# An mLSTM layer and its feed-forward block on one core: two groups' down projections change from float32 to divided float32r words, and the written order is new

## The chip, the cores and the metric

The kernel runs on one core of one Trainium2 chip. The metric is the device time of one execution in microseconds (us), the median of several runs. TensorE is called PE in the profile, its weight loads PEld, VectorE DVE, ScalarE ACT, GpSimd POOL, SyncE SP. All DMAs of the kernel are issued from SP's queue, in the order in which they are written.

## What is computed

Inputs are q, k, v and o_gate of shape (4, 8, 768, 40) and i_gate, f_gate of shape (4, 8, 768). For every batch and head, over the 768 time steps:

```
m_new = max(f + m, i);  f_stab = exp(f + m - m_new);  i_stab = exp(i - m_new)
C = f_stab * C + i_stab * outer(v, k);   n = f_stab * n + i_stab * k
y = sigmoid(o) * (C q) / max(|n q|, 1)
```

The result, as 3072 tokens of 320 values, goes through a feed-forward block with w_in (320 x 2048) and w_out (2048 x 320):

```
h = x @ w_in;   g = h * erf(softplus(h));   out = g @ w_out
```

The weights arrive as 64-bit words and are decoded on the chip.

## The kernel before

The sequence is cut into 12 chunks of 64 steps. For a chunk c, `attention` (line 414) works on two sides r of two batches each. For each side a scores step on PE (function `scores`, line 498), a heads step (`heads`, line 522) with the carried state (`before`, line 507), and short DVE steps give the chunk's y. The decay matrix `dm` is made for chunks 0 and 1 from a matmul `pb` (line 442) and an exponential on ACT (line 447); its operands are `lt` (line 338) and `xd` (lines 346 and 348), built once from the gates. Later chunks read the gates back from DRAM. `turned` (line 384) transposes y, `divided` (line 393) splits it into two float32r words, xh and xl, so that xh + xl is y.

The feed-forward block of a chunk's 256 tokens is done in four groups of 512 hidden columns, 48 groups in all, by `mlp(g)` (line 714). Groups 0 to 7 are those of chunks 0 and 1, alternating: groups 0, 2, 4, 6 are chunk 0's, 1, 3, 5, 7 chunk 1's. A group has two up steps of 16 matmuls (four of 5 from group 16 on), line 746, whose results ACT copies to `hb` (line 757); softplus and erf on ACT (lines 766, 770) and a product on DVE (line 774) give `n0`. Its down projection adds to two PSUM tiles, one for each half b of the tokens. It has two forms:

- undivided, for groups under PLAIN: for each half four float32 matmuls of n0 with the decoded w_out block `wo` (line 810). Each such matmul is recorded as two instructions.
- divided, for the other groups: `gh` is n0 in float32r (on ACT, line 784, for groups under 32), `gl` what is left of n0 (on DVE, line 790); w_out is divided into `woh` and `wol` by `split_out` (lines 707 and 711). For each half there are four matmuls gh x woh, four gh x wol (lines 814 and 815) and four gl x woh (line 812), in two steps of their own.

Nothing of this is ordered where it stands in the code: `Plan.add` records every step with its engine and what it reads and writes, and `Plan.run` issues the steps in a written list, `ORDER`, of the steps' numbers. Each engine executes its own steps in that order. A negative number -n in `ORDER` is a stay round: `stay(n)` issues n matmuls whose result is not used. `run` also puts in a load of an ACT function table (recorded at line 873) wherever a step on ACT needs a table that isn't loaded.

PSUM tiles of tag `pa` have two slots that are taken in turn by the steps of attention, the transposes and the down projections of chunk 1; `h` has two slots for up projections.

Of the kernel before, what the change touches and what calls it, by code (L numbers as in the profile page):

```python
# [33 lines left out]
class Plan:  # L34
# [131 lines left out]
PLAIN, JOIN, GH_ACT = 6, 3, 32  # L166
# [3 lines left out]
def tile_mlstm_moe(  # L170
# [43 lines left out]
    wl = cp.tile([128, 2, DFF], F32R, name="wl")  # L214
    woh = cp.tile([128, NFF, DM], F32R, name="woh")

    accs = []
    pob = [ps.tile([128, 512], F32, name=f"pob{b}") for b in range(2)]

    @dma(6, w=[('cst', 0)])  # L220
# [714 lines left out]
```

## Time and profile before

| | us |
|---|---|
| median of 3 runs | 464.68 (464.56 to 464.76) |
| the profiled execution | 462.74 |
| its span in the trace | 461.0 |
| PE busy | 450.4 |
| PE's weight loads busy | 402.8 |
| DVE busy | 330.7 |
| ACT busy | 336.9 |

The span is the time from the first to the last recorded event of the profiled execution. An engine's busy time is the time in which at least one of its instructions ran; ends of matmuls are modelled. The granted clock of PE is its mean over the span, 0.987 of full speed.

### The profile page before, as it was taken

What the parts mean: (1) busy time and instruction counts of PE and PEld (TensorE: products, weight loads), DVE (VectorE), ACT (ScalarE), POOL (GpSimd) and SP (SyncE); (2) the same over time, 40 slices, a digit from 0 to 9 for tenths busy, and PEclk for the clock granted to TensorE, in tenths of its full rate; (3) what the DMA queues carried; (4) which work ended last, traced back from release to release, by engine and by line L of the source; (5) the groups of instructions that cost most, each with busy time, mean ns of one, the idle gap of its engine ahead of it and who ended that gap; (6) DMA issues with size and microseconds to landing.
All of it is one profiled execution on the core that took longest, in us unless ns stands there. A gap on an engine that the chain in (4) does not pass through costs nothing.

```text
span 461.0 us, 14089 instructions
## 1 busy us (share of the span) xinstructions
PE 450.4 (98%) x6102; PEld 402.8 (87%) x6102; DVE 330.7 (72%) x655; ACT 336.9 (73%) x529; POOL 37.2 (8%) x62
## 2 busy tenths in 40 slices
PE   6989999999999999999999999999999999999996
PEld 4568998798889998999999899898899899999996
DVE  5879787857769477686868768858759876666491
ACT  4737999988878975786876895698596573575570
POOL 2000121020500200031000200102002000000000
PEclk9969999999999999999999999999999999999999
DMA  7999898923442141525317211672122300001011
GB/s 270 319 290 271 224 261 234 249 99 92 96 125 66 42 108 24 164 68 169 84 37 229 63 26 43 176 208 68 45 77 70 77 1 14 16 1 30 2 28 30
DMA packets 46831, 51.82 MB, mean 112 GB/s; under 512 B 27056, under 2 KB 31664, under 8 KB 46768
## 3 DMA queue, kind: packets, MB, share of 16 engines
q1 hardware_dynamic: 46768, 50.91, 39.8%
q8 instruction: 48, 0.79, 0.7%
q14 instruction: 15, 0.12, 0.1%
HBM read 46.77 MB, written 4.13 MB: 110 GB/s over the span
## 4 chain that ended last, share of the span: by engine, by line
PE 93%; DVE 3%; ACT 1%; issue 1%; DMA 0%; DVEq 0%
PE h L746 39%; PE pob L812 11%; PE pob L814 11%; PE pob L815 10%; PE pa L528 4%; PE pob L810 3%; PE pa L810 3%; PE pa L514 3%; PE pa L505 3%; PE pa L519 2%; PE pa L387 2%; PE pob L281 1%; PE pob L870 1%; PE pa L391 1%; DVE raw L633 1%
## 5 line engine op out<-in xcount | busy, mean ns | idle before, releaser
L746 PE MATMUL h<-xh,wh 128*128 128x256 f32 (+1 forms) x768 | 201.8, 345 | 0.2 <-ACT hb L757 0.2
L746 PEld LDWEIGHTS h<-xh,wh 128*128 128x128 f32 x768 | 126.5, 190 | 14.2 <-ACT hb L757 0.4
L757 ACT ACTIVATE hb<-h 128x256 f32<-128x256 f32 (+1 forms) x160 | 66.5, 423 | 66.0 <-PE h L746 65.2
L746 PE MATMUL h<-xh,wl 128*128 128x256 f32 x384 | 108.3, 282 | 0.0
L814 PE MATMUL pob<-woh,gh 128*128 128x320 f32 x328 | 98.3, 311 | 0.0
L815 PE MATMUL pob<-wo,gh 128*128 128x320 f32 x328 | 97.5, 309 | 0.0
L762 DVE TENSOR_TENSOR hb<-h,hb 128x256 f32<-128x256 f32 x128 | 52.6, 421 | 53.0 <-ACT hb L757 52.2
L873 ACT ACT_TABLE_LOAD x61 | 78.3, 1283 | 1.9 <-PEq L923 0.8
L746 PEld LDWEIGHTS h<-xh,wl 128*128 128x128 f32 x384 | 72.9, 190 | 2.2
L774 DVE TENSOR_TENSOR n<-n,hb 128x1024 f32<-128x1024 f32 x48 | 58.8, 1226 | 9.5 <-ACT n L770 9.5
L815 PEld LDWEIGHTS pob<-wo,gh 128*128 128x128 f32 x328 | 61.6, 188 | 1.5
L814 PEld LDWEIGHTS pob<-woh,gh 128*128 128x128 f32 x328 | 61.7, 188 | 0.4
L812 PE MATMUL pob<-woh,gl 128*128 128x320 f32 x328 | 61.7, 312 | 0.0
L483 POOL TENSOR_SCALAR_AFFINE_SELECT dm<-dm 128x512 f32<-128x512 f32 (+1 forms) x40 | 33.8, 851 | 310.9 <-ACT dm L463 229.4
L766 ACT ACTIVATE n<-hb 128x1024 f32<-128x1024 f32 x48 | 50.0, 1056 | 5.5 <-DVE hb L762 4.7
L812 PEld LDWEIGHTS pob<-woh,gl 128*128 128x128 f32 x328 | 52.3, 188 | 1.9
L790 DVE TENSOR_TENSOR gl<-n,gh 128x1024 fp32r<-128x1024 f32 x42 | 51.0, 1219 | 1.2 <-PE pob L815 0.4
L770 ACT ACTIVATE n<-n 128x1024 f32<-128x1024 f32 x48 | 49.9, 1055 | 0.3
L404 DVE TENSOR_TENSOR xh<-pa,xh 128x384 fp32r<-128x384 f32 x24 | 13.2, 551 | 23.1 <-ACT xh L400 23.0
L784 ACT ACTIVATE gh<-n 128x1024 fp32r<-128x1024 f32 x26 | 27.2, 1053 | 0.0
L560 DVE TENSOR_TENSOR dm<-pa,dm 128x512 f32<-128x512 f32 x24 | 16.4, 685 | 10.7 <-PE pa L505 7.6
L820 ACT ACTIVATE o<-pob 128x320 f32<-128x320 f32 x22 | 9.5, 437 | 17.4 <-PE pob L812 17.4
(97 smaller groups left out, 484.6 us busy)
## 6 DMA issues: line engine op xcount, KB each, us to landing
qk<-in_qk_dram SPq DMA_DIRECT2D x24, 512.0 KB
kvo<-in_kvo_dram SPq DMA_DIRECT2D x24, 484.0 KB
eT<-gd SPq DMA_DIRECT2D x44, 128.0 KB
raw<-in_w_out_dram SPq DMA_DIRECT2D x16, 320.0 KB
dm<-gd SPq DMA_DIRECT2D x40, 128.0 KB
raw<-in_w_in_dram SPq DMA_DIRECT2D x8, 512.0 KB
out_dram<-o SPq DMA_DIRECT2D x48, 80.0 KB
raw<-in_w_in_dram SPq DMA_DIRECT2D x4, 256.0 KB
```

Of the source, the lines that this page charges most:

```text
L483: nc.gpsimd.affine_select(out=x, in_=x, pattern=[[0, H], [1, L]], compare_op=ALU.is_ge, fill=0.0, base=base, channel_multiplier=-1)
L746: nc.tensor.matmul(h[:, n * T:n * T + n_], w, m, start=(s == 0), stop=(s == len(ops) - 1))
L757: nc.scalar.activation(part(), G(f'h{i}')[:, T:2 * T] if wide else G(f'h{i}'), AF.Copy)
L762: nc.vector.tensor_tensor(part(), G(f'h{i}')[:, 0:T], part(), op=ALU.add)
L766: nc.scalar.activation(new('n0', [128, 1024], ('n0', g)), G('hb'), AF.Softplus)
L770: nc.scalar.activation(G('n0'), G('n0'), AF.Erf)
L774: nc.vector.tensor_tensor(G('n0'), G('n0'), G('hb'), op=ALU.mult)
L790: nc.vector.tensor_tensor(new('gl', [128, 1024], ('gl', g), F32R), G('n0'), G('gh').bitcast(F32), op=ALU.subtract)
L812: nc.tensor.matmul(acc(b), G('gl')[:, ts], woh[:, j], start=False, stop=(j == NFF - 1))
L814: nc.tensor.matmul(acc(b), G('gh')[:, ts], woh[:, j], start=(j == 0), stop=False)
L815: nc.tensor.matmul(acc(b), G('gh')[:, ts], t['wol', j], start=False, stop=False)
L873: plan.run(ORDER, lambda k: nc.scalar.preload_act_table_set(KIND[k]), stay)
```

## The change

PLAIN goes from 6 to 4, so that the down projections of groups 4 and 5 take the divided form, and the division of w_out's blocks 8 to 11 is needed by them. ORDER is replaced as a whole; it has 1595 steps in place of 1587, numbered anew, and stay rounds that add up to six, as before. A stay round that comes before any down projection now multiplies the identity if that has been made, and the zeroed state otherwise, so that it can stand ahead of the step that makes the identity.

```diff
 ORDER = [
-    1, 2, 0, 5, 9, 4, 6, 12, 13, 14, 3, 10, 7, 15, 16, 99, 101, 20, 31, 8, 17, 11, 33, 100, 102, 32, 34, 36, 35, 27, 28, 93,
-    95, 19, 38, -1, 40, 42, -2, 47, 341, 342, 18, 26, 30, 48, 343, 49, 50, 94, 96, 103, 67, -1, 68, 25, 37, 24, 39, 105, 23,
...
+    1, 4, 0, 3, 5, 7, 9, 11, 12, 6, 13, 2, 14, 15, 16, 8, 17, 33, 27, 32, 34, 36, 35, 20, 19, 31, 38, -1, 40, 28, 26, 29, 93,
+    95, 349, 350, 351, 42, -2, 47, 94, 48, 49, 18, 67, 68, 99, 96, 10, 50, 59, 60, 25, 37, 30, 39, 52, 65, 23, 100, 101, 102,
...
 ]
-PLAIN, JOIN, GH_ACT = 6, 3, 32
+PLAIN, JOIN, GH_ACT = 4, 3, 32
...
-    accs = []
+    accs, made = [], []
...
         make_identity(nc, ident)
+        made.append(ident)
...
-                nc.tensor.matmul(pob[1], ident, ident.unsqueeze(1).to_broadcast([128, 4, 128]), start=True, stop=True)
+                x = made[0] if made else state[0].rearrange("p j n d -> p (j n d)")[:, 0:128]
+                nc.tensor.matmul(pob[1], x, x.unsqueeze(1).to_broadcast([128, 4, 128]), start=True, stop=True)
```

Read through the step numbers, the first PE steps are, with pb, S, H for the decay matmul, scores and heads, the chunk and the side behind them, T for transposes, A for the transposition of the gates (line 358) and up for an up step:

```
old: warm pb01 pb00 S01 stay1 H01 stay2 pb11 stay1 S00 pb10 T01 H00 stay1 S11 S10 stay1 T00 A  H11 up0 up2 up2
new: warm pb01 pb00 S01 stay1 H01 stay2 pb11 pb10 S00 T01 H00 stay2 S11 S10 stay1 A T00 H11 up0 up2 up2
```

The first ACT steps around the exponentials of line 447 are:

```
old: ... exp01 tanh01 exp00 decode(i00) xd state01 lt decode ...
new: ... exp01 tanh01 exp(gates) xd exp00 tanh00 decode(i00) state01 lt ...
```

The down projections of groups 0 to 7 stand further apart in the new list: groups 0 and 2 first, then up steps of groups 8 to 11, then groups 1, 3, 5 and 7 close together, then 4 and 6.

## Rows read from the trace of the kernel before

**Rows 1.** The page's first part: busy us, share of the span, instructions.

```profile
PE 450.4 (98%) x6102; PEld 402.8 (87%) x6102; DVE 330.7 (72%) x655; ACT 336.9 (73%) x529; POOL 37.2 (8%) x62
```

**Rows 2.** Windows: stretch, length, busy us by engine, PE clock, DMA share, GB/s.

```profile
0.00:44.00 44.00, 37.46 (x674) 26.50 (x674) 32.72 (x79) 24.81 (x56) 3.37 (x22) 0.88 0.97 288
44.00:457.00 413.00, 412.96 (x5430) 376.32 (x5429) 297.96 (x578) 311.62 (x472) 33.78 (x40) 1.00 0.35 94
...
0.00:126.00 126.00, 119.42 (x1873) 98.69 (x1874) 95.35 (x217) 100.43 (x172) 18.11 (x38) 0.96 0.78 218
...
455.00:461.00 6.00, 2.00 (x14) 1.73 (x12) 0.00 (x0) 0.57 (x2) 0.00 (x0) 0.89 0.25 55
```

**Rows 3.** Waits of PE over the whole span: total us, times, longest.

```profile
PE pob L281 <- DVE sel L258: 3.6, 1, 3.6
PE pa L505 <- issue: 1.9, 1, 1.9
```

**Rows 4.** Windows of 1 us around 25 to 38 us.

```profile
24.00:25.00 1.00, 0.00 (x0) 0.00 (x0) 0.94 (x2) 0.00 (x0) 0.00 (x0) 1.00 1.01 397
...
26.00:27.00 1.00, 1.00 (x2) 0.30 (x2) 1.00 (x2) 0.00 (x0) 0.00 (x0) 0.62 1.07 427
...
37.00:38.00 1.00, 1.00 (x11) 1.00 (x10) 0.91 (x5) 0.85 (x3) 0.00 (x0) 1.00 1.01 308
```

**Rows 5.** PE's timeline, undivided down projections and what follows: start, us.

```profile
67.21 2.32 PE L810 MATMUL pob<-wo,n 128*128 128x320 f32 x8
69.46 0.69 PE L505 MATMUL pa<-qk 40*64 40x64 f32 x32
...
90.08 4.57 PE L810 MATMUL pa<-wo,n 128*128 128x320 f32 x16
94.50 0.53 PE L358 MATMUL pa<-ident,x 128*128 128x32 f32 x4
```

**Rows 6.** PE's timeline, first of 12 divided matmuls and what follows them.

```profile
98.61 0.31 PE L814 MATMUL pa<-woh,gh 128*128 128x320 f32 x1
...
100.38 0.40 PE L746 MATMUL h<-xh,wh 128*128 128x256 f32 x2
```

**Rows 7.** Groups by line: busy us, mean ns, idle before.

```profile
L873 ACT ACT_TABLE_LOAD x61 | 78.3, 1283 | 1.9 <-PEq L923 0.8
...
L790 DVE TENSOR_TENSOR gl<-n,gh 128x1024 fp32r<-128x1024 f32 x42 | 51.0, 1219 | 1.2 <-PE pob L815 0.4 <-PE pob L812 0.4 <-ACT gh L784 0.3
...
L784 ACT ACTIVATE gh<-n 128x1024 fp32r<-128x1024 f32 x26 | 27.2, 1053 | 0.0
```

**Rows 8.** ACT's timeline from 9.6 us.

```profile
9.69 0.60 ACT L447 ACTIVATE dm<-pa 128x512 f32<-128x512 f32 x1 [1.21 <-PE pa L442]
10.18 0.46 ACT L488 ACTIVATE kvo<-kvo 128x320 f32<-128x320 f32 x1
10.54 0.60 ACT L447 ACTIVATE dm<-pa 128x512 f32<-128x512 f32 x1
...
11.59 2.01 ACT L346 ACTIVATE xd<-x,heads_of 128x64 f32<-128x64 f32 x8
```

**Rows 9.** PE's timeline: heads steps, a decay matmul, a scores step's last part.

```profile
12.12 0.66 PE L519 MATMUL pa<-vg,kvo 64*64 64x41 f32 x32
...
17.71 1.13 PE L442 MATMUL pa<-xd,lt 128*128 128x512 f32 x2
...
19.88 0.66 PE L519 MATMUL pa<-vg,kvo 64*64 64x41 f32 x32
...
25.50 0.34 PE L505 MATMUL pa<-qk 40*64 40x64 f32 x6 [1.92 <-issue]
```

**Rows 10.** PE's timeline in the first up step, 12 matmuls between the two.

```profile
33.54 0.41 PE L746 MATMUL h<-xh,wl 128*128 128x256 f32 x1
...
36.10 0.41 PE L746 MATMUL h<-xh,wh 128*128 128x256 f32 x1
```

**Rows 11.** The chain that ended last, in order of time: one later up step.

```profile
74.15 1.91 PE h L746 x16
```

137 rows, old and new, of the table ORDER are left out of this document.

## The prediction

> **What bounds the kernel now.** I read the shares of the engines first. TensorE (PE) is busy for 98% of the span, VectorE (DVE) and ScalarE (ACT) for some 72% [rows 1]. An average can hide a stage with another limit, so next come the windows [rows 2]: from 44 to 457 us PE is busy for 412.96 of 413 us at full granted clock. Before 44 it is busy 37.46 of 44 us at a mean clock of 0.88, with the DMA engines 97% busy. After 457 comes only the last eviction and its store: PE is busy 2.00 of the last 6 us. "Busy" is a modelled duration for pipelined matmuls, so the windows alone don't show that PE works at its peak; the distances between the starts of matmuls do, in the part below. The waits of PE [rows 3] add up to 6.4 us, all before 44 us; the two largest are shown, and one is the wait for the first data. The other, 1.9 us, waits for nothing that the profile shows. So two things set the time: how long PE's own list of work takes from 44 us on, and how soon, and at which clock, PE gets going before that.
>
> The 1 us windows show the opening's weak place [rows 4]. PE does nothing from 24 to 25 us, the granted clock is 0.62 in 26 to 27, stays at its lower level (0.50, 1.2 GHz), and is back at 1.00 in 37 to 38.
>
> **The change, part by part.**
>
> *Removed and added on PE.* Groups 4 and 5 lose their undivided down projections. The undivided form is 8 float32 matmuls of 320 columns a group, each recorded as two instructions. Group 5 ran as one block of 16 instructions from 90.08 to 94.50, 4.42 us. Group 4 ran in halves; a half of 8 instructions takes 2.25 us (67.21 to 69.46, that of group 0), so 4.50 us [rows 5]. Together 8.92 us. In their place come 12 float32r matmuls for each half of the tokens: 8 with gh (lines 814, 815) and 4 with gl (line 812). Group 7 did such a half from 98.61 to 100.38, 1.77 us [rows 6]; four halves are 7.08 us. The difference is 8.92 - 7.08 = 1.84 us less on PE, 0.92 a group. PE has no idle time there, so I count all of it. Its bounds: 1.76 if both groups had cost 4.42, 1.92 if both had cost 4.50.
>
> The Trainium skill (FP8 and Floating Point Precision, TensorE Precision Notes) says that true float32 takes four passes through the array. By that rule alone three single passes in place of four would save a quarter of 8.92, 2.2 us, and the time would be 462.4; the rows say 1.84, since a float32r matmul takes somewhat more than a quarter of a float32 one.
>
> *Added on ACT and DVE.* Two more gh copies on ACT at 1.053 us, two more gl subtractions on DVE at 1.219 us [rows 7]. Following both written orders through the planner's rule for activation tables gives 61 loads for the old order, as many as the trace has, and 54 for the new one: seven fewer, at 1.283 us 9.0 us less on ACT [rows 7]. ACT thus loses 9.0 - 2.1 = 6.9 us net, DVE gains 2.4. Neither engine is the bound after 44 us, so I cost both at nothing. What hides them is PE's full list; what it costs when that cover is gone is a rival below. The steps that divide w_out are the same 16; those of blocks 8 to 11 only move ahead of group 4's and 5's projections.
>
> *The order of the opening.* Up to the first up projection both orders give PE the same steps, five stay rounds included, and ask for the same qk, kvo and w_in loads, within some 16 KB. Two things differ. First, the exponential of the second side's decay (line 447) ran on ACT at 10.54, before the 2.01 us that build the second half of xd; the new order puts it behind them and behind another tanh [rows 8]. Counted from the first exponential's end: 10.29 + 0.46 + 2.01 + 0.60 = 13.36. The first heads step needs the PSUM slot that this exponential frees, and started at 12.12 [rows 9]. It will start about 1.2 us later. Second, the new order puts pb of the fourth side directly behind that of the third, ahead of the scores, and drops one stay round between them, so a step that PE did late before (17.71) now fills what was a wait. I reckon that the lag has shrunk by the heads step at 19.88, but can't price it exactly: its bounds are 0 and 1.2 us. Then comes PE's gap, whose end (25.50, the last 6 matmuls of a scores step of 32 pairs) no data releases [rows 9]: it falls inside one step whose first 26 pairs had run, and the new order reaches it after the same PE steps. I expect it again, at nearly the same time, and hiding what is left of the lag. So I take 0.
>
> *pA2 ahead of the transposes.* In the new order the small transposition of the gates (line 358) precedes the transposes of chunk 0's second side. The next step then takes its PSUM slot after a short ACT copy instead of after the division by ACT and DVE. PE waited only 0.2 us there, so this gives at most 0.2; I take 0.
>
> *The first groups.* For its second pair of up projections the new order wants w_in's second tail as well, because DVE decodes it earlier: about 0.5 MB more than before. At the 288 GB/s of the first 44 us [rows 2] that is 1.8 us of transfer, but later steps want about 1 MB less than before at the same place. PE is doing the first up projection meanwhile. Bounds: 1.8 lost, nothing lost; I take nothing.
>
> *The end.* After group 47's last up projection the new order leaves PE twelve pieces of down projection (groups 44 to 46, 3 x 3.54 = 10.6 us) before it needs group 47's. The old order leaves as much. No change.
>
> Sum: 464.68 - 1.84 = 462.84, say 462.8. The profiled execution took 462.74 (span 461.0, with 1.7 around it), 1.94 below the median of the runs; I add the difference to the median, and for a profiled run of the new kernel would expect 460.9.
>
> **The rivals.**
>
> *The opening becomes shorter.* At the lower clock the up projection's matmuls started every 0.213 us (12 of them from 33.54 to 36.10 [rows 10]); at the higher one a step of 16 takes 1.91 us, 0.119 each [rows 11]. So an up step costs 1.5 us more at the lower clock. If the activity before 26 us changes so that the clock falls later or returns one step earlier, 462.84 - 1.5 = 461.3; with one and a half steps 460.6. For it: the new order closes gaps between 15 and 19 us. Against: the gap at 24 us has the same PE steps before it.
>
> *The lag of 1.2 us is carried through.* Then 464.0, and with a further wait for the second tail up to 465.6: no measurable change. For it: ACT's list really has the 2.01 us in front. Against: PE's later gap is longer than the lag.
>
> *DVE falls behind between 90 and 130 us; slower.* The new order packs DVE's work tighter there: eight divisions of w_out and the gl of groups 5 and 7 come close together. Adding the mean durations of all DVE instructions that stand in the new order ahead of what the scores of chunk 4's first side need, scaled by 0.92 so that a whole kernel's sum equals DVE's busy time, gives 100.1 us. PE's list puts those scores at 127.5, so DVE may have idled 27.4 us by then. The old kernel's DVE had idled 126 - 95.35 = 30.65 us by 126 [rows 2], its order allowing 33.7. If DVE idles as it did, PE waits 3.3 to 3.5 us: 462.84 + 3.5 = 466.3. It decides from 2.8 us of waiting on. Against: DVE idled mostly waiting for ACT, and ACT has fewer table loads now; the same count for ACT leaves 27.6 us or more where the old kernel idled about 25.6 [rows 2].
>
> *The lower clock lasts two up steps longer; slower, barely.* Two steps at 1.5 are 3.0 us: 465.8. This happens if PE idles again between 33 and 40 us, waiting for w_in. The windows show what precedes a fall: a microsecond without matmuls, then 0.62 [rows 4]. The Trainium skill (TensorE: Matmul & The Clock Gate, Part 1) says that the clock is released by PE's activity and taken back when it idles; the trace agrees, with 0.00 us of PE work in 24 to 25 and 0.50 soon after.
>
> **How the numbers follow.** Forecast (1.84 less, the opening even to within 0.9): 0.46, 461.9 to 463.7. Shorter opening: 0.17. Lag carried: 0.20. DVE late: 0.11. Lower clock longer: 0.06. This kernel's runs lie within 0.05% of each other; 0.2%, 0.93 us, is about what can be told from no change. Faster by more than that, below 463.75: 0.46 + 0.17 = 0.63. Within it: 0.20. Slower, above 465.61: 0.17. The range runs from 460.6 (a shorter opening by one and a half steps) to 466.3 (DVE late by 3.5); some 0.15 lies outside.
>
> **What would show it.** Right: 32 fewer float32 down instructions (line 810), 64 in all; 54 table loads; PE busy in practically every window after 46 us; the last matmul some 1.8 us earlier; a gap without a releaser in the second scores step of chunk 1 near 25 us, with the clock falling after it. Wrong: PE waits named DVE or ACT between 60 and 140 us, or a first dense stretch that starts more than 1 us before or after 44.

## The result, and the profile after

The changed kernel takes 459.06 us (median of 4 runs, 458.40 to 460.07), against 464.62 before: ratio 0.9882, 95% interval 0.9863 to 0.9901. It is 5.6 us faster; 1.84 was forecast, and 459.06 lies below the range. The profiled execution took 458.40 with a span of 456.7, 4.3 less than before. The rest up to 5.6 is the old kernel's profiled execution lying 1.9 below its median, the new one's 0.7. All lines of the code stand two or three further down now (746 is 748, 810 is 812, 505 is 507, 528 is 530, 873 is 876).

The page's first part, and from its third part PE's instruction queue (packets, MB, share):

```profile
PE 445.6 (98%) x6118; PEld 401.6 (88%) x6118; DVE 336.5 (74%) x657; ACT 328.5 (72%) x524; POOL 37.3 (8%) x62
...
q8 instruction: 48, 0.79, 0.7%
```

Windows of the changed kernel, with columns as in [rows 2]:

```profile
0.00:44.00 44.00, 37.13 (x702) 27.36 (x703) 35.12 (x86) 28.36 (x63) 3.34 (x22) 0.96 0.88 281
...
40.50:456.70 416.20, 411.96 (x5457) 377.71 (x5445) 304.62 (x580) 303.64 (x469) 33.96 (x40) 1.00 0.34 97
...
29.00:30.00 1.00, 0.05 (x5) 0.04 (x7) 0.97 (x3) 0.84 (x2) 0.00 (x0) 1.00 0.63 156
31.00:32.00 1.00, 1.00 (x9) 1.00 (x8) 0.97 (x2) 0.86 (x2) 0.00 (x0) 0.65 0.75 251
37.00:38.00 1.00, 1.00 (x11) 1.00 (x10) 0.94 (x3) 0.92 (x2) 0.00 (x0) 1.00 0.99 399
```

PE was as busy in the first 44 us as before, but at a mean clock of 0.96 in place of 0.88 [rows 2]. The dense stretch begins near 40.5, not at 43.9. Waits of PE over the whole span (total, times, longest):

```profile
PE pob L283 <- DVE state L272: 3.6, 1, 3.6
PE pa L530 <- issue: 1.8, 1, 1.8
PE pa L507 <- issue: 0.9, 2, 0.7
PE h L748 <- DVE wl L649: 0.2, 1, 0.2
```

The one wait of 1.9 us without a releaser [rows 3] has become several, of which PE's timeline shows the two largest; it answers to [rows 9]:

```profile
11.59 0.66 PE L521 MATMUL pa<-vg,kvo 64*64 64x41 f32 x32
...
18.48 0.66 PE L521 MATMUL pa<-vg,kvo 64*64 64x41 f32 x32
19.07 0.81 PE L530 MATMUL pa<-kvo,dm 64*32 64x41 f32 x64
...
22.03 1.11 PE L507 MATMUL pa<-qk 40*64 40x64 f32 x58 [0.23 <-issue]
23.84 0.34 PE L507 MATMUL pa<-qk 40*64 40x64 f32 x6 [0.70 <-issue]
...
27.47 0.65 PE L530 MATMUL pa<-kvo,dm 64*32 64x41 f32 x46
29.95 0.38 PE L530 MATMUL pa<-kvo,dm 64*32 64x41 f32 x18 [1.83 <-issue]
30.26 0.51 PE L748 MATMUL h<-xh,wh 128*128 128x256 f32 x2
```

I cut both traces at the same work: the start of the first up matmul, the start of the fourth up step (the same steps lie before it in both), and the start of the last block of gl matmuls.

| us | before | after | difference |
|---|---|---|---|
| gap inside the two scores steps ends | 25.50 | 23.84 | -1.66 |
| first up matmul | 32.95 | 30.26 | -2.69 |
| fourth up step | 43.94 | 40.53 | -3.41 |
| last gl block | 456.25 | 451.91 | -4.34 |
| from the fourth up step to the last gl block | 412.31 | 411.38 | -0.93 |

Each trace is one execution. So 3.41 of 4.3 us came ahead of the stretch for which the prediction counted a gain, from a part it costed at nothing. After that it is 0.93, not 1.84. These are the two things to explain.

### The profile page after: what moved, and what is told of

Its sections match the earlier page's. It is cut to its first block, busy times and chain, and to the rows that moved or that the text cites. A ratio compares the mean times of both kernels' runs of the same rounds, so it can differ in the third digit from the quotient of the medians.

```text
span 456.7 us, 14133 instructions
## 1 busy us (share of the span) xinstructions
PE 445.6 (98%) x6118; PEld 401.6 (88%) x6118; DVE 336.5 (74%) x657; ACT 328.5 (72%) x524; POOL 37.3 (8%) x62
## 4 chain that ended last, share of the span: by engine, by line
PE 92%; DVE 3%; ACT 2%; DMA 1%; issue 1%; SPq 0%; DVEq 0%
PE h L748 40%; PE pob L816 11%; PE pob L814 11%; PE pob L817 11%; PE pa L530 3%; PE pa L507 3%; PE pa L516 3%; PE pa L812 2%; PE pob L812 2%; PE pa L521 2%; PE pa L389 2%; PE pa L444 1%; PE pob L873 1%; DMA eT<-gd 1%; DMA gt<-in_gates_dram 1%
## 5 line engine op out<-in xcount | busy, mean ns | idle before, releaser
L816 PE MATMUL pob<-woh,gh 128*128 128x320 f32 x336 | 101.1, 313 | 0.0
L817 PE MATMUL pob<-wo,gh 128*128 128x320 f32 x336 | 100.1, 310 | 0.0
L817 PEld LDWEIGHTS pob<-wo,gh 128*128 128x128 f32 x336 | 63.2, 188 | 1.4
L816 PEld LDWEIGHTS pob<-woh,gh 128*128 128x128 f32 x336 | 63.2, 188 | 0.5
L814 PE MATMUL pob<-woh,gl 128*128 128x320 f32 x336 | 62.7, 312 | 0.0
L792 DVE TENSOR_TENSOR gl<-n,gh 128x1024 fp32r<-128x1024 f32 x44 | 53.9, 1228 | 2.2 <-ACT gh L786 1.9
L814 PEld LDWEIGHTS pob<-woh,gl 128*128 128x128 f32 x336 | 53.5, 188 | 2.0
L786 ACT ACTIVATE gh<-n 128x1024 fp32r<-128x1024 f32 x28 | 29.5, 1052 | 0.0
L530 PEld LDWEIGHTS pa<-kvo,dm 64*32 64x32 f32 x1536 | 16.7, 106 | 5.9 <-issue 5.0
```

The lines of the kernel that those rows point to most:

```text
L792: nc.vector.tensor_tensor(new('gl', [128, 1024], ('gl', g), F32R), G('n0'), G('gh').bitcast(F32), op=ALU.subtract)
L814: nc.tensor.matmul(acc(b), G('gl')[:, ts], woh[:, j], start=False, stop=(j == NFF - 1))
L816: nc.tensor.matmul(acc(b), G('gh')[:, ts], woh[:, j], start=(j == 0), stop=False)
L817: nc.tensor.matmul(acc(b), G('gh')[:, ts], t['wol', j], start=False, stop=False)
```

## The experiments

All kernels compute the whole reference. The old kernel ran beside them on other chips: 464.3 to 464.6 us in the median, single runs from 461.2 to 466.3. Ratios are to those runs. A few figures come back:

- *dense*: from the fourth up step to the last gl block.
- *at the lower clock*: from windows of 1 us between 20 and 46, twice the sum of (1 - granted clock), so that a window at 0.50 counts as 1 us.
- *packet*: a 16 KB transfer of the queue q8, which moved 48 of them. PE has 6118 matmul and 6118 load records, 12236 instructions; divided by 256 that is 47.8. A packet holds 256 of PE's instructions.

**The projections alone (a1_new6).** The new order with six groups undivided.

```diff
-PLAIN, JOIN, GH_ACT = 4, 3, 32
+PLAIN, JOIN, GH_ACT = 6, 3, 32
 ORDER: gh and gl of groups 4 and 5 dropped, their down steps joined,
        the division of w_out's blocks 8 to 11 behind them, all else in place
```

> The new written order with groups 4 and 5 undivided again: PLAIN is 6, the steps gh and gl of these groups are left out, each half is one float32 step where its gh step stood, and the division of w_out's blocks 8 to 11 comes after them. Theory (opening and projections are two separate gains): the first up step starts at 30 us as in the new kernel, and the time is 1.84 us (the sum of the prediction) or at least 0.9 us (what the distance from the fourth up step to the last gl block shrank by) above the new kernel's 459.06: 460.0 to 460.9. Rival (the divided projections gave it all): 464.6, as before the change.

460.87 us, ratio 0.9931 (0.9904 to 0.9959). The windows over the dense stretch, of this kernel, the new one and the old one:

```profile
40.12:453.38 413.26, 412.74 (x5433) 376.13 (x5426) 301.88 (x579) 301.62 (x466) 31.38 (x40) 1.00 0.34 97
...
40.53:451.91 411.38, 411.19 (x5450) 377.23 (x5442) 304.62 (x580) 303.17 (x468) 33.96 (x40) 1.00 0.34 97
...
43.94:456.25 412.31, 412.27 (x5426) 375.90 (x5426) 298.02 (x578) 311.62 (x472) 33.78 (x40) 1.00 0.35 94
```

Dense is 413.26, against 411.38 with the divided form: 1.88 us, of which 0.3 is one wait for DVE that only this kernel has there. By PE's busy time alone it is 412.74 - 411.19 = 1.55. The step of 1.84 was right to within 0.3. Its opening is as short as the new kernel's (fourth up step at 40.12), so the short opening belongs to the order and not to PLAIN. Against the old order's 412.31 the new one costs 0.95 more in the dense stretch; 0.5 of that is PE idle (412.74 busy of 413.26, before practically none), the other 0.5 longer busy time for the same steps, and why is not shown.

**The order cut in two (a2_newopen_old, a3_oldopen_new, c1_newopen50, c2_oldopen50, c5_newopen_old4).** One order up to a cut and the other behind it; the cut is the first up step (a2, a3) or the scores of chunk 2's second side, near 50 us (c1, c2, c5). The new kernel ran again beside them (c0_after).

```diff
 a2:  new order to the cut | old order, six groups undivided
 a3:  old order to the cut | new order, four groups undivided
 c1, c2: as a2, a3 with the later cut;  c5: as c1 with four groups undivided
```

> The new order's steps up to the first up step, then all others in the old order, groups 4 and 5 undivided: only the opening is changed. Theory (the opening's order gave 3.4 us): 461.2, first up step near 30.3 us. Rival (the order after the opening, or the projections, gave the time): 464.6, whatever the opening does.

> The old order's steps up to the first up step, then all others in the new order, groups 4 and 5 divided. Theory (opening and rest are separate): the old opening's 464.62 less the 0.9 to 1.84 us of the projections, 462.8 to 463.7, first up step near 33 us. Rival (the rest of the new order gave the time): 459 to 460.

> The new kernel itself again, beside kernels that mix its order with the old one. Its opening varies from run to run with the first loads: 458 to 460.5, fourth up step near 40 to 41 us, 411.4 us from there to the last gl block.

> The new order's steps through the scores of chunk 2's second side (near 50 us), then the old order; groups 4 and 5 undivided. Theory (the new opening, with the loads and decodes that belong to it, gives 3.4 us): 461.2, and 412.3 us from the fourth up step to the last gl block, as in the old order. Rival (the joint, not the order, made the earlier mixed kernel slow only by chance, and the opening is worth nothing by itself): 464.4.

> The old order's steps through the scores of chunk 2's second side, then the new order; groups 4 and 5 divided. Theory: no gain of the opening, 411.4 us from the fourth up step to the last gl block, so 463.5. Rival (the later order gives the time): 459 to 460.

> The new order's steps through the scores of chunk 2's second side, then the old order with groups 4 and 5 divided: their gh and gl beside group 7's, the division of blocks 8 to 11 ahead of them, the down projections of groups 5 and 7 just ahead of the scores of chunk 3's first side. Theory (the new list after the opening costs PE some 0.9 us by itself, against the old list, which the divided projections' 1.88 us hide): 410.4 us from the fourth up step to the last gl block and a time 0.9 us under the new kernel's, 458.2. Rival (the old list has no room on ACT and DVE for the added copies and divisions by 95 us): PE waits for gh, gl or woh near 90 to 105 us, and the time is no better than the new kernel's, 459 to 463.

c0_after repeats the result: 458.89, ratio 0.9884 (0.9865 to 0.9902). The old opening with the new rest gains nothing that is sure: a3 463.21, 0.9984 (0.9955 to 1.0013); c2 464.95, 1.0013 (0.9999 to 1.0027). Their fourth up steps stand at 45.32 and 47.27. They are no clean measure either: PE waits for hb, 1.8 us in a3 and 2.3 in c2, against 0.2 in the old kernel. The other direction is spoilt more: a2 465.50, 1.0025 (1.0002 to 1.0048); c1 473.12, 1.0174 (1.0156 to 1.0192); c5 481.23, 1.0353 (1.0335 to 1.0371). In c5 PE waits 5.2 us for an eviction on ACT (o) and 5.1 for hb, in c1 5.1 for hb and 2.8 for den: the lists of ACT and DVE don't fit each other across the cut. As a measure of the opening these three fail. a2 still shows that the new opening runs to its end as quickly (first up matmul at 28.94).

**Where the gap sits (b1_warm10, and b2_warm10_new in the new order).** The same columns ahead of everything in more instructions: ten matmul records more, each with its weight load, 20 instructions.

```diff
-        for _ in range(5):
-            nc.tensor.matmul(pob[1][:, 0:256], zeros[:, 0:128], zeros[:, 0:256], start=True, stop=True)
+        for _ in range(10):
+            nc.tensor.matmul(pob[1][:, 0:128], zeros[:, 0:128], zeros[:, 0:128], start=True, stop=True)
```

> The old kernel with its opening warm step cut differently: ten matmuls of 128 columns in place of five of 256, so that PE's list has 20 instructions more ahead of the same work. Theory (PE waits for the next block of its instruction list, which ends at a fixed count of instructions): the gap without a releaser in chunk 1's second scores step comes 10 pairs earlier, after about 48 of the 64 in place of 58. Rival (a transfer or a semaphore of that step holds it): still after 58, or gone.

> The changed kernel with the warm step's five matmuls of 256 columns as ten of 128: the same columns, 20 instructions more ahead of everything. Theory (blocks of a fixed number of instructions): the first gap comes 10 matmul records earlier, after 48 of the 64 of the two scores steps, and the second 10 earlier, after 36 of the 64 of the heads step, each 1.2 to 1.8 us behind the end of an instruction packet. Rival (the gap belongs to a place in the program: a buffer, a semaphore): after 58 and 46 again. Time within 2 us of the changed kernel's.

PE's timeline of b1_warm10 at the gap:

```profile
22.82 0.93 PE L505 MATMUL pa<-qk 40*64 40x64 f32 x48 [0.36 <-DMA qk<-in_qk_dram]
...
26.91 0.70 PE L505 MATMUL pa<-qk 40*64 40x64 f32 x16 [3.16 <-issue]
```

58 records have become 48: the gap moved by exactly the ten that were put in. It belongs to a count of instructions, not to a step, a buffer or a semaphore. In b2_warm10_new there is also a gap after 48 (0.48 us, behind one of 1.06 ahead of the two scores steps); the second, expected after 36 of the heads step, isn't there: that step began only at 30.07, at the lower clock, when its packet (27.1) had come. The times, one run each, were 466.60 and 459.53.

**What brings the gap's end.** The DMA view of the old kernel from 22.9 to 23.0 us and of the new one from 21.1 to 21.2, the tenths of a microsecond in which a packet starts:

```profile
q8 instruction: 1, 0.02, 70.1%
```

```profile
q8 instruction: 1, 0.02, 84.6%
```

A packet lies on one of 16 engines, so 70.1% of 16 x 0.1 us is 1.12 us: it lands at 24.0, and the gap ends at 25.50. In the new kernel: 21.1 + 1.35 = 22.5, and 23.84. In the same way, landings to within 0.2 us, one execution each, with the DMA share of the window from 20 to 22 us:

| kernel | second heads step (L528, L530) | DMA 20-22 | packet starts | lands | gap ends | gap | at lower clock | fourth up step |
|---|---|---|---|---|---|---|---|---|
| before | 20.47 | 1.24 | 22.9 | 24.0 | 25.50 | 1.92 | 10.2 | 43.94 |
| a3_oldopen_new | 20.28 | 1.24 | 23.6 | 24.7 | 26.21 | 2.82 | 10.2 | 45.32 |
| c2_oldopen50 | 20.72 | 1.18 | 25.8 | 26.9 | 28.27 | 4.43 | 10.2 | 47.27 |
| a4_pb10 | 20.79 | 1.25 | 24.6 | 25.8 | 27.18 | 2.59 | 3.4 | 46.02 |
| d1_hold | 20.27 | 1.08 | 22.8 | 24.1 | 25.39 | 1.96 | 3.4 | 44.17 |
| e1_early | 19.75 | 1.04 | 23.2 | 24.4 | 26.15 | 2.60 | 13.6 | 45.84 |
| after | 19.07 | 0.67 | 21.1 | 22.5 | 23.84 | 0.70 | 3.4 | 40.53 |
| c0_after | 19.59 | 0.67 | 21.8 | 23.0 | 24.49 | 0.62 | 0.0 | 40.83 |
| a1_new6 | 18.99 | 0.72 | 21.1 | 22.2 | 23.62 | 0.42 | 0.0 | 40.12 |

In all nine PE goes on 1.3 to 1.7 us after the packet lands. The new kernel's second gap does too: packet from 27.6 to 28.6, end at 29.95. The gap starts where the instructions end that PE has, and ends with the next packet. The block before it begins with the second heads step (64 records of it, two or four of stays and 58 of scores lie between); PE runs through it in 3.1 to 4.3 us. The packet starts 2.0 to 2.2 us after that step where the DMA engines were 0.67 to 0.72 busy, and 2.4 to 5.1 where they were full.

Five further traces with the new opening bear on this. In a2, c1, c5 and f2 (DMA share 0.62 to 0.89) the packet started 0.8 to 1.7 us after the step and had landed by 22.1 at the latest, and there the gap does not occur at all. In b2_warm10_new, with a share of only 0.73, it started 2.8 us after the step. A late packet and the gap thus go together in every trace; the share from 20 to 22 us alone does not say how late the packet is.

The gap is also not the whole wait, only what the block's own work leaves of it. From the second heads step to the gap's end it takes 5.03 us before and 4.77 after, 0.26 less, while the gap shrank by 1.22 (1.92 to 0.70). Another 0.23 are idle ahead of the scores now, and the rest is filled by the stay round, which has four records in this block in place of two (1.99 us for 1.12). a4_pb10 and e1_early have the four as well, and with their late packets their gaps are 2.59 and 2.60: the stay round alone does not close it.

**The transfers put back (e1_early).** In the old kernel SP's queue asks for the third w_in tile (512 KB) at 17.32 and for the fourth and fifth from 20.04. SPq's timeline of the old kernel:

```profile
17.32 1.45 SPq L655 DMA_DIRECT2D raw<-in_w_in_dram  x1
...
20.04 1.26 SPq L655 DMA_DIRECT2D raw<-in_w_in_dram  x2
```

In the new one the queue stands at a small write of the gates, as its waits from 15 to 24 us show, and asks for the third and fourth from 22.53:

```profile
SPq L379 <- ACT x L372: 2.9, 1, 2.9
```

```profile
22.53 0.85 SPq L657 DMA_DIRECT2D raw<-in_w_in_dram  x2
```

Here, in the new kernel, the two are put ahead of the eT transfers and are issued from 16.75:

```profile
16.75 1.89 SPq L656 DMA_DIRECT2D raw<-in_w_in_dram  x2
```

```diff
 SP's queue
+   w_in 3rd tile, w_in 4th tile
    eT of chunk 1's second side (2 DMAs), write of the gates
-   w_in 3rd tile, w_in 4th tile
    write of the gates, w_in second tail (2 DMAs)
```

> The new kernel with the third and fourth w_in loads put ahead of the first read-back of the gates in SP's queue, so that the DMA engines stay full from 18 to 24 us as before the change; all else is the new order. Theory (full DMA engines make the instruction block late): from the second heads step to the end of the gap 5 to 7.5 us in place of 4.6 to 4.9, a lower clock for longer, time 0.5 to 3 us above the new kernel's, 459.5 to 462. Rival: 458.9, or less, because the weights come earlier.

461.66 us, ratio 0.9944 (0.9923 to 0.9965): of the 1.16% that the change gained, 0.60%, 2.8 us, are gone again. Its windows, and PE's timeline at the gap:

```profile
20.00:22.00 2.00, 2.00 (x64) 1.12 (x51) 1.93 (x7) 1.33 (x4) 0.00 (x0) 1.00 1.04 415
...
24.00:26.00 2.00, 0.00 (x0) 0.00 (x0) 0.83 (x2) 0.00 (x0) 0.00 (x0) 0.81 0.93 177
```

```profile
22.41 1.14 PE L506 MATMUL pa<-qk 40*64 40x64 f32 x58
26.15 0.49 PE L506 MATMUL pa<-qk 40*64 40x64 f32 x6 [2.60 <-issue]
```

The gap is long again (2.60 for 0.70), PE does nothing from 24 to 26, the clock falls from 25 on, and dense is 411.29, as in the new kernel (411.38). (This profiled execution, 463.62, was the slowest of its 12, so the trace shows more of the loss than the median.) The opening gained 3.4 us in the two traces and 4.6 by the medians (5.6 less the 0.93 of the dense stretch). In the new order the transfers' place alone thus takes back 2.8 of that, more than half. The loss of time is that of 12 runs; that it comes about by the late packet is read from this one trace, in which PE has no wait above 0.2 us for another engine behind the first.

Asking later has a price too. The third and fourth tiles are read by the second up step, and in c0_after PE waits there for their divided parts:

```profile
PE h L748 <- DVE wl L649: 1.0, 1, 1.0
PE h L748 <- ACT wh L645: 0.4, 1, 0.4
```

In a1_new6 it is 0.9 and 0.5 us, in the new kernel's first trace, where the clock fell, 0.2. So c0_after, with no time at the lower clock, reaches its fourth up step no earlier (40.83 for 40.53).

**The same tried in the old order (d1_hold).** The exponential of the gates and its write moved so that the third to fifth w_in tiles are asked for from 23.76 us.

```diff
 ACT's list, SP's queue
-   exp(gates of chunk 2), write of the gates, ... copy of w_in's first tail
+   copy of w_in's first tail, ... exp(gates of chunk 2), write of the gates
    (SP) w_in 3rd to 5th tile behind that write
```

> The old order with two things moved: the exponential of the second gate block stands behind the first division of w_in's tail on ACT, and the write of its result to DRAM stands ahead of the third w_in load in SP's queue, so that this load and all behind it start near 23 us in place of 17 to 20. Theory (the block of instructions lands late because the DMA engines are full): from the second heads step's own matmuls to the end of the gap 4.6 to 4.9 us in place of 5.0 to 7.6, clock lower for less than 5 us in place of 10, time 462 to 463.5. Rival (only the time at which PE reaches the step matters): 5 us or more as before, and 464.6 or more, since w_in comes later.

463.63 us, ratio 0.9996 (0.9973 to 1.0019): a miss. The hold was put too late for this block: the DMA engines were still full from 20 to 22 (1.08) and free only from 22 to 24 (0.31), when the packet, at 22.8, was about to start; the gap stayed at 1.96. What the opening gained after the gap was lost to later data: PE waits for wh (0.56) and hb (1.15), and dense is 413.60. That later transfers gain something in the old order is thus not shown.

**The earlier arrival alone (a4_pb10, d2_arrive, d3_both).** The new kernel reaches its second heads step 1.4 us earlier. In the old order a4 puts pb and exponential of the fourth side behind those of the third; d2 also moves load and decode of the second w_in tile behind the first gate loads; d3 adds d1's hold.

```diff
-stay1 H01 stay2 pb11 stay1 S00 pb10 T01 H00 stay1 S11
+stay1 H01 stay2 pb11 pb10 S00 T01 H00 stay2 S11
 (d2, d3)  second w_in tile: its load and its decode on ACT and DVE later
```

> The old order with one thing of the new opening: the decay matmul of the fourth side and its exponential stand directly behind those of the third, and the stay round between moves behind the next heads step. Theory (this one move lets PE reach the second scores step of chunk 1 some 1.4 us earlier, so that its gap without a releaser ends earlier and the clock falls later): first up step 1.5 to 2.7 us earlier, 461.9 to 463.2. Rival (the clock's fall hangs on something else in the opening): within 0.5 us of 464.6.

> The old kernel with the arrival alone changed: the second w_in tile's load and decode stand behind the first gate loads, and pb of the fourth side with its exponential stands directly behind pb of the third. Theory (the second heads step begins earlier, so the next block of instructions is asked for earlier, but the DMA engines are as full as before): second heads step at 19 to 20 us in place of 20.47, the gap still 1.5 to 4 us long and the clock falling, 463.0 to 465.5 us. Rival (the arrival is what the change gained, the DMA engines' load nothing): 461.0 to 461.6 us with a gap that ends by 24 us.

> The last kernel with the new order's start as well: the second w_in tile's load and decode wait behind the first side's data, the fourth side's decay matmul and exponential follow the third's, and the stay round between stands behind the next heads step. Theory (earlier arrival and a free DMA queue together are the new opening): second heads step near 19 us, gap ends near 23.8, first up step near 30 to 31, time 461 to 462, that is 464.6 less the opening's 3.4. Rival (the weights' order matters more): PE waits for wh, wl or hb after the first up step, and 463 or more.

a4: 464.68, 1.0005 (0.9980 to 1.0029), with the second heads step at 20.79, not earlier. d2: 467.13, 1.0065 (1.0041 to 1.0090). d3: 468.65, 1.0095 (1.0063 to 1.0126). Waits of PE in d2:

```profile
PE pa L505 <- ACT dm L447: 2.7, 1, 2.7
PE pa L442 <- DVE kvo L599: 2.1, 1, 2.1
```

pb10 now stands in front of the scores and waits for DVE, and the scores for the exponential behind it; the second heads step came at 25.09 (d3: 25.49). None of the three made the arrival earlier, so they say nothing of what it is worth.

**The second gap (f2_tail).** The new kernel with the second tail of w_in (2 x 256 KB) behind the fifth tile.

```diff
 SP's queue, and the decode of the tail on ACT and DVE
-   w_in second tail, eT, w_in 5th tile
+   eT, w_in 5th tile, w_in second tail
```

> The changed kernel; only the load of w_in's second tail (two DMAs of 256 KB) and its decode stand later, behind the load and decode of the fifth w_in tile. Theory (PE's instructions arrive in blocks of 16 KB through the same DMA engines; a block is late when they are full): the DMA engines have about 0.5 MB less to move around 24 to 27 us, the second block's packet starts earlier than 27.6 us and the gap inside the heads step (1.83 us in the changed kernel) shrinks by 0.5 to 1.2 us: 458.0 to 458.6 us, unless the tail is then late for the second pair of up steps, which would show as a wait of PE for wh or wl between 33 and 40 us. Rival (the gap has a fixed length, whatever the DMA engines do): a gap of 1.8 us again, and 459.0 us or more.

461.99 us, ratio 0.9948 (0.9927 to 0.9968). The packet starts at 27.2 for 27.6, and the gap in the heads step is 1.20 for 1.83, but this shows nothing for the theory: in c0_after, the new kernel unchanged, they are 27.5 and 1.20. And the waits of PE have these too:

```profile
PE pa L515 <- DVE qe L477: 2.1, 1, 2.1
...
PE pa L388 <- DVE kvo L606: 0.9, 1, 0.9
```

The fourth up step starts at 42.87. DVE's decode stands in a list that qe and kvo share; the fourth up step comes 2.3 us later. No run beat the new kernel.

## Why the prediction was wrong

**What bounds the kernel: right.** PE's list and the opening set the time; the clock in the opening was the weak place.

**Projections, -1.84: right as a step.** In the new kernel a group's divided projections run as one block here, first and last row of PE's timeline, from the first of its 24 matmuls to the next group's:

```profile
108.33 0.55 PE L816 MATMUL pa<-woh,gh 128*128 128x320 f32 x1
...
112.12 0.31 PE L816 MATMUL pa<-woh,gh 128*128 128x320 f32 x1
```

That is 3.79 with the step into it, 3.40 for the 23 from its second matmul on (108.72), or 3.55 for 24 at that pace; 3.54 was counted. a1_new6 measures 1.88 for both groups, 1.55 of it in PE's busy time. What I did not count is that the new list itself costs 0.95 in the dense stretch, so that 0.93 is left of it.

**ACT and DVE at nothing: right.** These lines answer to [rows 7]:

```profile
L876 ACT ACT_TABLE_LOAD x54 | 69.3, 1283 | 1.7 <-PEq L926 0.8
...
L792 DVE TENSOR_TENSOR gl<-n,gh 128x1024 fp32r<-128x1024 f32 x44 | 53.9, 1228 | 2.2 <-ACT gh L786 1.9
...
L786 ACT ACTIVATE gh<-n 128x1024 fp32r<-128x1024 f32 x28 | 29.5, 1052 | 0.0
```

54 loads as counted, ACT 8.4 us less busy (6.9 counted), DVE 5.8 more (2.4 counted), and behind 40.5 us PE waits for them 0.2 us in all.

**The opening at 0: the step that failed**, in both its halves. First the lag. ACT's timeline has the second exponential where I put it, behind xd:

```profile
9.15 0.60 ACT L449 ACTIVATE dm<-pa 128x512 f32<-128x512 f32 x1 [1.37 <-PE pa L444]
...
10.21 2.00 ACT L348 ACTIVATE xd<-x,heads_of 128x64 f32<-128x64 f32 x8
12.11 0.58 ACT L449 ACTIVATE dm<-pa 128x512 f32<-128x512 f32 x1
```

But the first heads step ran at 11.59, before that exponential began, and behind DVE's product of the scores, which it reads:

```profile
10.67 0.69 DVE L562 TENSOR_TENSOR dm<-pa,dm 128x512 f32<-128x512 f32 x1 [0.39 <-PE pa L507]
```

It did not need the slot which I had it wait for; there was no lag of 1.2 us. The two slots of `pa` are not taken strictly in turn, as I had written: with the exponential still to come, the step can only have had the slot of the scores, free since that product. [Rows 8, 9] did not show such a wait either: the exponential had ended at 11.14, the step began at 12.12, behind a stay round that PE had begun at 11.06, and I read the order of two events as a dependence.

Second, "I expect it again, at nearly the same time". The gap came again after the same PE steps, 58 of 64 records, but ended 1.66 us earlier, and the clock did not fall after it, only after the second gap, at 31 us. I took a wait without a releaser for something fixed. It is the wait for PE's own next instructions, which the profile counts on the same 16 DMA engines as w_in, and a change of SP's queue changes it (e1_early: 2.60 us for 0.70, and 2.8 us of time). 1.40 of the 1.66 us is the second heads step's earlier start (19.07 for 20.47), 0.26 the shorter time from there to the gap's end. With the short gap the clock stays at 1.00 until 31 us: from the gap's end to the first up matmul it takes 6.42 us with 1.83 of another gap inside, against 7.45 without one. I asked of the opening how many bytes are loaded, and not when. My own sign of being wrong, a dense stretch that starts more than 1 us before 44, came true. A smaller slip: the new order has four stay rounds there and not five, with six matmuls as before.

The Trainium skill (Runtime: NRT & Kernel Launch, Instruction fetch mechanics) says that an engine fetches its instructions by a DMA queue of its own, in 16 KiB blocks of 256 instructions, while it runs the block before, and that the cost is mostly hidden. The trace agrees on the size (48 packets for 12236 instructions) and for the dense stretch, where PE has no such wait; in the opening it does not, with 0.4 to 4.4 us.

**pA2, first groups, the end: right, as nothing.** PE waits 0.2 us for wl (1.4 for wl and wh in c0_after; these are parts of the third and fourth tiles, not of the tail that I had priced); the last gl block stands 4.79 us before the span's end, 4.75 before the change.

**The rivals.** A shorter opening had 0.17 and is what happened, though I put its reason in the clock alone and its price at 1.5 to 2.2 us. No lag, no DVE behind at 90 to 130 us, no longer stretch at the lower clock came. (The lag's upper price is mis-added: 464.0 and 1.8 are 465.8, not 465.6.)

**What stays open.** e1_early takes back 2.8 us of the 3.4 (traces) to 4.6 (medians) that the opening gained. How the rest divides between the earlier arrival, the stay round in the block and chance is not settled, since no kernel changed one of them alone. Nor do these runs show why a packet starts as late as it does under load: 2.4 to 5.1 us after the heads step at shares of 1.04 to 1.25.

## What to carry to other kernels

A wait of PE without a releaser, in the middle of a run of small matmuls while the DMA engines are full, should be looked up in the rows of the instruction queue before it is taken as fixed: here it ends 1.3 to 1.7 us after a packet of 256 instructions lands. When an order is rewritten, compare when each queue issues its large transfers, not only how many there are; two tiles of 512 KB, asked for 5.8 us later in SP's queue (16.75 and 22.53), were worth more here (2.8 us) than two groups' cheaper projections (1.55 to 1.88). And an order is one piece: ten of the eleven kernels here that cut it or shifted a part of it (all but e1_early) made PE wait elsewhere, for 1.7 us or more.

## What the runs showed of the hardware

- PE can run out of instructions. A block of some 127 matmul records with their loads, nearly all of 41 or 64 columns, took PE 3.1 to 4.3 us in the opening; in the nine kernels of the table the next one came 4.6 to 7.6 us after the block's start. In the dense stretch 256 instructions last 412.27 x 256 / (5426 + 5426) = 9.7 us on the mean, and no such wait is seen.
- After a gap of 0.4 to 0.7 us the clock did not fall; it fell after gaps of 1.83 us and more in the rows above, for 3.4 to 13.6 us, and not after second gaps of 1.20 (c0_after) and 1.3 us (a1_new6). In b2_warm10_new it fell from 25 us on behind two of 1.06 and 0.48 us that lay 1.4 us apart.
- The old kernel's runs on other chips spread over 461.2 to 466.3 us, at granted clocks of 0.983 to 1.000 over the span. Whether the opening makes them vary is not shown: none of them has a trace here.
